# VectorE exp as a sum of four shifted bit patterns, two-tile ScalarE steps, and three shared PSUM banks, in a fused attention and feed-forward kernel

## The chip, the cores and the metric

One core of a Trainium2 chip runs the whole program. The metric is the device time of one execution in microseconds (us); several executions are taken and their median is given. The kernel before takes 830.55 us (three runs, 829.79 to 830.59). Each execution also has the mean clock that was granted to TensorE, as a share of full speed, and a state: fast, or slow when it is over 1.5% above the fastest run of the same kernel. Comparisons below are of fast runs, unless a line says otherwise.

## The reference, cut to what matters

```python
xn = _layernorm(x)                                  # x: 1 x 2048 x 640
q = (xn @ wq) -> 32 heads of 20; k = xn @ wk; v = xn @ wv     # one k and v for all heads
p = softmax(einsum("bhqd,bkd->bhqk", q, k) * 20 ** -0.5)
attention = (p @ v) @ wo
h = relu(xn @ w1 + b1); ffn = (h * h) @ w2 + b2               # 640 -> 1536 -> 640
return x + attention + ffn
```

The dominant work is exp of 32 x 2048 x 2048 scores. The kernel cuts it into 2,048 tiles of 128 x 512 (keys x queries of one head).

## The kernel before

ScalarE computes exp with its own function for most tiles. VectorE takes the rest and approximates exp through the bits of a bf16 number: a scaled score plus an offset, written as uint16 and read as bf16, is a piecewise linear 2^x. The kernel before corrects that line with a quadratic in the mantissa, in passes over four tiles (128 x 2048) at a time, called a set:

```python
# before, one set (L: bits of four tiles; n: number of the set)
d1   = DVE: lbuf[u16] = score * XA + XB                 # 4 times, from PSUM, 128x512
wop  = DVE: wbuf[u16] = (L & 0xFF80) | 124              # 128x2048
uop  = DVE: ubuf[u16] = (L & 0x7F) | 0x3F80
t1   = DVE: T = L * ubuf
t2   = DVE or (every other set) POOL in two halves: T = T * ubuf
# value products: 3 matmul groups a set: (lbuf, v), (wbuf, 0.5 v), (T, 0.164 v)

ACT_BANKS = ((0, 1, 2), (3, 4))   # ScalarE steps: 3 tiles, 2 tiles, 3 tiles, ...
DBANKS = (5,)                     # scores for VectorE
PVB = 6                           # value products
MB = 7                            # everything else ("misc": projections, feed-forward, output)
SQ (square of the feed-forward): POOL
```

The order of instructions on every engine is not written by hand. At build time a planner in the kernel simulates the engines with a duration for every operation, and emits what it would start first; on the chip each engine is given its list in that order, with semaphores. When the plan has nothing for TensorE it puts in fillers (matmuls with a zero weight, which add nothing), to keep TensorE's clock up:

```python
# for each engine: the ready operations; the earliest start wins, then priority
if pick[2].eng == "PE":
    while pick[0] > free["PE"] + 0.1 + ... and pe_credit(free["PE"]) < 0.0:
        commit(Op("fill", "PE", 0.215, [... zeros32 ...]))     # pe_credit falls with FILL * time
```

In row tiling (scores: contraction over 20 rows, four heads in four row tiles) and in column tiling (all else: 32 output columns, four column tiles) TensorE does up to four small matmuls at a time, a column group (in the timeline of the kernel before, at 401.57 us, four that start together are done in 0.39 us; one alone, at 407.72 us, takes 0.38). Matmuls write to PSUM, which the kernel uses as eight banks of 128 x 512. (`...` marks cuts.)

The softmax here doesn't subtract the row's maximum and nothing guards it: scores larger than these inputs give would overflow.

Of the kernel before, what the change touches and what calls it, by code (L numbers as in the profile page):

```python
# [13 lines left out]
HPG = 4  # L14
G = H // HPG
NBLK = QC * G
NQS = 4
# [8 lines left out]
CC = 0.1640625  # L26
LOG2K = -1.1033179
XA = SCALE * 1.4426950408889634 * 128.0
XB = (127.0 - EXP_SHIFT * 1.4426950408889634 + LOG2K) * 128.0

PTR = 20
ACT_BANKS = ((0, 1, 2), (3, 4))
DBANKS = (5,)
# [3 lines left out]
T2POOL = (0, 1)  # L37
DLEAD = 14.0
DGAP = 0.5
SWITCH = 0.1  # L40
FILL = 0.7

# [48 lines left out]

class Op:
# [3 lines left out]
    def __init__(self, name, eng, dur, parts, deps=(), toks=(), lat=0.06, lock=False, mode="C"):  # L96
        self.name, self.eng, self.dur, self.parts = name, eng, dur, parts
        self.deps = [d for d in deps if d is not None]
        self.toks = list(toks)
        self.lat, self.lock, self.mode = lat, lock, mode  # L100
        self.start = self.fin = None
        self.consumed = False
        self.tgt = None
        self.clock = None

    def ready(self):
        t = 0.0
        for d in self.deps:
            if d.fin is None:
                return None  # L110
            t = max(t, d.fin + d.lat)
        return t


def bass_parallel_sum__grouped_kv_mqa__dense_activation_squared_relu__prompt_kernel(nc, A_x, A_wq, A_wk, A_wv, A_wo, B_x, B_w1, B_b1, B_w2, B_b2, out):
    es = ExitStack()
    with es:
# [11 lines left out]
        stats6 = sb("stats6", [128, ST, 2, 6], F32)  # L129
# [11 lines left out]
        vxh = sb("vxh", [128, KT, 32], BF16)  # L141
        vxc = sb("vxc", [128, KT, 32], BF16)
# [3 lines left out]
        T2 = sb("T2", [128, 2, 512], BF16)  # L146
        OTn = sb("OTn", [128, 2, G, 512], BF16)
# [6 lines left out]
        ones0 = sb("ones0", [128, 128], BF16)  # L154
# [3 lines left out]
        part = sb("part", [128, 4, D], F32)  # L158
# [3 lines left out]
        tbuf = sb("tbuf", [128, 2, SETW], BF16)  # L162

        xfree = x_sb[:, :, :].rearrange("p st d -> p (st d)")
        lbuf = xfree[:, 0:2 * SETW].rearrange("p (a n) -> p a n", a=2)
        wbuf = xfree[:, 2 * SETW:4 * SETW].rearrange("p (a n) -> p a n", a=2)
        ubuf = sb("ubuf", [128, 2, SETW], BF16)
# [220 lines left out]
        def em_pool_consts():  # L388
            add(P.pool, lambda e: e.memset(ones0[:], 0.0), inc=c_pool)
            add(P.pool, lambda e: e.memset(ones0[0:1, :], 1.0), waits=[(c_pool, c_pool.n)], inc=c_pool)  # L390
# [182 lines left out]
        def add_scaled_v(c):  # L573
            cs = slice(4 * c, 4 * c + 4)
            d_, t_ = need_chunk(4 * c, v_op)
            o1 = Op(f"VH{c}", "POOL", 0.25, [lambda e: e.tensor_scalar(out=vxh[:, cs, :], in0=vx[:, cs, :], scalar1=0.5, scalar2=None, op0=ALU.mult)], d_, t_, lock=True)
            o2 = Op(f"VC{c}", "POOL", 0.25, [lambda e: e.tensor_scalar(out=vxc[:, cs, :], in0=vx[:, cs, :], scalar1=CC, scalar2=None, op0=ALU.mult)], d_, t_, lock=True)
            pool_q.extend([o1, o2])
            vs_op[c] = (o1, o2)
# [10 lines left out]
        mb_last = [None]  # L590

        def col4(lhs, rhs, n, k, last, m=32, bank=MB):
            return [mm(ps[32 * j:32 * j + m, bank, 0:n], lhs(j), rhs, k == 0, last, (0, 32 * j)) for j in range(4)]

        def unit_T(st):
            def chunk():
                return [(lambda e, dt=dt: e.transpose(out=psbf(MB)[:, dt * 128:(dt + 1) * 128], in_=xn_sb[:, st, dt * 128:(dt + 1) * 128], identity=ident[:])) for dt in range(DT)]  # L597

            def evac(p):
                o = Op(f"TE{st}", "DVE", 0.49, [lambda e: e.tensor_copy(out=xnT[:, :, st * 128:(st + 1) * 128],  # L600
                                                                        in_=psbf(MB)[:, 0:DT * 128].rearrange("p (dt n) -> p dt n", dt=DT))], [p])
# [4 lines left out]
        def unit_KT(c):  # L606
# [3 lines left out]
            def evac(p):  # L610
                o = Op(f"KTe{c}", "DVE", 0.75, [lambda e: e.tensor_scalar(out=kT[:, 512 * c:512 * (c + 1)], in0=ps[:, MB, :], scalar1=nk0[:, 1:2], scalar2=None, op0=ALU.add)],  # L611
# [5 lines left out]
        def unit_V(c):  # L617
            sts = range(4 * c, 4 * c + 4)

            def chunk():  # L620
                r = []
                for st in sts:
                    for dt in range(DT):
                        r.append(lambda e, st=st, dt=dt: e.matmul(ps[:, MB, DH * (st % 4):DH * (st % 4) + DH], xnT[:, dt, st * 128:(st + 1) * 128], wv_c[:, dt, :],  # L624
# [3 lines left out]
            def evac(p):  # L628
                o = Op(f"Ve{c}", "DVE", 0.24, [lambda e: e.tensor_copy(out=vx[:, 4 * c:4 * c + 4, 0:DH], in_=ps[:, MB, 0:4 * DH].rearrange("p (t d) -> p t d", t=4))],
# [7 lines left out]
        def unit_B1():  # L637
            def evac(p):
                b1_ev[0] = Op("B1e", "DVE", 0.17, [lambda e: e.tensor_copy(out=b1col[:], in_=psbf(MB)[:, 0:FT])], [p])
                return b1_ev[0]  # L640
            return Unit("B1", [(0.2, lambda: [lambda e: e.transpose(out=psbf(MB)[:, 0:FT], in_=b1row[:, :], identity=ident[0:FT, 0:FT])])],
                        lambda: True, evac, lambda: [], [(b1_sem, 16), (c_pool, v_ident)])

        def unit_QT(b):
# [5 lines left out]
            def evac(p):  # L650
                o = Op(f"QTe{b}", "DVE", 0.66, [lambda e: e.tensor_copy(out=qT[:, b % NQS, :], in_=ps[:, MB, :])], [p] + list(q_users.get(b - NQS, [])))  # L651
# [8 lines left out]
        def unit_FFN1(qc, f):  # L660
# [4 lines left out]
            def evac(p):  # L665
                k = nffn[0]
                nffn[0] += 1
                o = Op(f"RL{qc}_{f}", "DVE", 0.75, [lambda e: e.tensor_scalar(out=hT_tmp[:, k % 2, :], in0=ps[:, MB, :], scalar1=b1col[:, f:f + 1], scalar2=0.0,  # L668
# [8 lines left out]
                q = Op(f"SQ{qc}_{f}", "POOL", 1.15, [lambda e: e.tensor_tensor(out=h2T[:, qc % 2, f, :], in0=hT_tmp[:, k % 2, :], in1=hT_tmp[:, k % 2, :], op=ALU.mult)], dp, tk, lock=True)  # L677
                ffn_sq.append(q)
                sq_op[(qc, f)] = q
                pool_q.append(q)  # L680
# [5 lines left out]
        def out_mats(qc, st, half, gs, with_ffn):  # L686
# [3 lines left out]
            if with_ffn:  # L690
                for f in range(FT):
                    mats.append((h2T[:, qc % 2, f, stl * 128:(stl + 1) * 128], w2_sb[:, f, cs]))
                mats.append((ones0[:, :], b2pad[:, cs]))
# [4 lines left out]
        def out_chunks(mats, bank=MB, first=True, last=True):  # L698
            n = len(mats)
            ch = []  # L700
            for k, (l, r) in enumerate(mats):
                kk = k if first else k + 1
                ch.append((0.14, (lambda kk=kk, k=k, l=l, r=r: col4(lambda j: l[:, 32 * j:32 * j + 32], r, 320, kk, last and k == n - 1, 32, bank))))
# [22 lines left out]
        def unit_OUT(qc, st, half):  # L726
# [3 lines left out]
            def evac(p):  # L730
                o = Op(f"OE{st}_{half}", "DVE", 0.49, [lambda e: e.tensor_tensor(out=out_sb[:, slot, cs], in0=ps[:, MB, 0:320], in1=xr[:, slot, cs], op=ALU.add)],  # L731
# [13 lines left out]
        def unit_OUTP(st, half):  # L745
# [3 lines left out]
            def evac(p):  # L749
                o = Op(f"OP{st}_{half}", "DVE", 0.49, [lambda e: e.tensor_tensor(out=part[:, st % 4, cs], in0=ps[:, MB, 0:320], in1=xr[:, st % 4, cs], op=ALU.add)],  # L750
# [46 lines left out]
        act_tiles = []  # L797
# [6 lines left out]
        sets, steps = [], []  # L804

# [19 lines left out]
        def blk_qk_done(b):  # L825
            return cur["b"] > b and all(not (s["b"] == b and s["left"]) for s in sets) and all(st_["qk"].fin is not None for st_ in steps if any(t[0] == b for t in st_["tiles"]))

        def make_step():
            j = len(steps)
            banks = ACT_BANKS[j % 2]  # L830
            tl, (b1_, kt1, h1), rest = peek_tiles(len(banks))
            if not tl or not all(kt_ok(kt) and (b == 0 or b in qt_op) for b, kt, h in tl):
                return None
            cur["b"], cur["kt"], cur["h"] = b1_, kt1, h1
            for b, r in rest.items():
                unclaimed[b] = r
            i0 = len(act_tiles)
            st_ = dict(j=j, tiles=tl, banks=banks, i0=i0, act=None)
            steps.append(st_)
            act_tiles.extend(tl)  # L840
            parts, deps, toks = [], [], []
            for k, (b, kt, h) in enumerate(tl):
                for d_, t_ in (need_chunk(kt, kt_op), need_q(b)):
                    deps += d_
                    toks += t_
                parts.append(mm(ps[:, banks[k], :], kT[32 * h:32 * h + DH, kt * 128:(kt + 1) * 128], qT[32 * h:32 * h + DH, b % NQS, :], True, True, (32 * h, 0)))
            if j < 2:
                toks += all_pro
            st_["qk"] = Op(f"QK{j}", "PE", 0.215, parts, deps, toks, lat=0.2, mode="R")
            for (b, kt, h) in tl:  # L850
                q_users.setdefault(b, []).append(st_["qk"])
            return st_

        def act_can(st_):
            return all(i < PTR or act_tiles[i - PTR][:2] in pv_of for i in range(st_["i0"], st_["i0"] + len(st_["tiles"])))

        def make_act(st_):
            i0, n = st_["i0"], len(st_["tiles"])
            s0 = i0 % PTR
            deps = [st_["qk"]] + [pv_of[act_tiles[i - PTR][:2]] for i in range(i0, i0 + n) if i >= PTR]  # L860
            b0 = st_["banks"][0]
            return Op(f"ACT{st_['j']}", "ACT", 0.064 + 0.4267 * n, [lambda e: e.activation(out=PT[:, s0:s0 + n, :], in_=ps[:, b0:b0 + n, :], func=AF.Exp, bias=-EXP_SHIFT, scale=SCALE)], deps)  # L862

        def after_act(st_):
            for k, t in enumerate(st_["tiles"]):
                tile_act[t] = (st_["act"], (st_["i0"] + k) % PTR)
# [5 lines left out]
        def make_pv(b, kt):  # L872
# [11 lines left out]
            return Op(f"PV{b}_{kt}", "PE", 0.215, parts, deps, toks, lat=0.2)  # L884

        def make_dpv(s):
            b, kt, term, n = s["b"], s["kt"], s["term"], s["n"]
            first, last = b not in pv_begun, pv_count[b] == KT - 1 and term == 2
# [407 lines left out]
```

## Time and profile before

| | before |
|---|---|
| median | 830.55 us |
| span of the profiled run | 840.8 us |
| score tiles on ScalarE / VectorE | 1,696 / 352 |
| ScalarE exp steps | 339 of three tiles, 339 of two, 1 of one |
| filler matmuls | 1,088 |

In the views PE is TensorE, PEld its weight loads, DVE is VectorE, ACT ScalarE and POOL GpSimd; L12 is line 12 of the kernel. The profiled run of the kernel before is one of its longer ones (clock 0.962), so its span is above the median. From the page of the kernel before: busy time of each engine with its share of the span; TensorE's granted clock in 40 slices, in tenths; the chain that ended last.

```profile
PE 775.6 (92%) x10439; PEld 254.9 (30%) x10439; DVE 678.5 (81%) x973; ACT 794.5 (94%) x724; POOL 268.4 (32%) x168
...
PEclk8689999987989999999999999999999999999999
...
ACT 61%; PE 28%; DVE 6%; issue 1%; DVEq 0%
```

ScalarE is the bound, with TensorE next. Groups of the same page follow: line, engine, operation, what it writes and reads, count | busy us, mean ns of one | idle us of the engine just before it, and what ended that.

```profile
L862 ACT ACTIVATE PT<-ps 128x1536 bf16<-128x1536 f32 (+1 forms) x679 | 775.0, 1294 | 29.3 <-PE ps L549 27.5
...
L978 DVE TENSOR_SCALAR x_sb<-ps 128x512 uint16<-128x512 f32 x352 | 241.3, 685 | 113.2 <-PE ps L549 110.7
...
L549 PE MATMUL ps<-kT,zeros 128*32 128x512 bf16 x1088 | 87.9, 401 | 0.0
...
L985 DVE TENSOR_SCALAR x_sb<-x_sb 128x2048 uint16<-128x2048 uint16 x88 | 68.6, 780 | 0.5
```

The exp group is 775 us busy with 29 us of idle time before it. Mean durations overlap (the next step starts before the last one has ended), so I used start-to-start times: 1.330 us for three tiles, 0.903 us for two.

Two more lines are from the views of two lines of the source: GpSimd's own work with one input. Columns: engine, operation, tiles, count, duration in ns least/median/longest, first and last start, form.

```profile
L307 POOL TENSOR_SCALAR big<-x_sb,rstd,nmr x9: 868/874/1034, 10.4 to 23.5; 128x640 bf16<-128x640 bf16 x9
```

```profile
L576 POOL TENSOR_SCALAR vxh<-vx x4: 527/528/612, 28.8 to 58.7; 128x128 bf16<-128x128 bf16 x4
```

The first is the normalisation, the second one multiplication by a constant, at widths of 640 and 128.

### The profile page before, as it was taken

How to read it: one execution, taken by the hardware profiler on the slowest of the kernel's cores; microseconds unless marked ns; L12 is line 12 of the kernel's file. 1: busy time of each engine (PE TensorE's matmuls, PEld its weight loads, DVE VectorE, ACT ScalarE, POOL GpSimd, SP SyncE). 2: the span in 40 equal slices, each digit the busy share in tenths (PEclk: the TensorE clock that was granted, in tenths of full speed). 3: DMA queues.
4: the chain of work that ended last, by engine and by line, in shares of the span. 5: the costliest groups of instructions: out<-in, count | busy, mean ns of one | idle time of the engine just before them, and what ended most of it. 6: DMA issues, size and time to landing. Idle time of an engine off the chain costs nothing.

```text
span 840.8 us, 22953 instructions
## 1 busy us (share of the span) xinstructions
PE 775.6 (92%) x10439; PEld 254.9 (30%) x10439; DVE 678.5 (81%) x973; ACT 794.5 (94%) x724; POOL 268.4 (32%) x168
## 2 busy tenths in 40 slices
PE   7799999999999999899999999999899999999996
PEld 3232222222223333222223333322222333323332
DVE  5768888776878888889887877889888888888874
ACT  7589999997989999999999999999899999999995
POOL 4424344531222321254432223135343232223221
PEclk8689999987989999999999999999999999999999
DMA  9500000000000000000000000000000000000000
GB/s 306 120 2 2 1 2 2 2 2 1 2 2 17 3 17 18 17 2 2 2 2 2 17 18 17 3 16 2 2 2 2 18 17 18 17 2 2 3 2 33
DMA packets 11714, 14.94 MB, mean 18 GB/s; under 512 B 2017, under 2 KB 10978, under 8 KB 11618
## 3 DMA queue, kind: packets, MB, share of 16 engines
q1 hardware_dynamic: 10306, 13.44, 5.2%
q8 instruction: 81, 1.33, 0.7%
q10 hardware_dynamic: 1312, 0.05, 0.1%
q14 instruction: 15, 0.12, 0.0%
HBM read 10.87 MB, written 2.62 MB: 16 GB/s over the span
## 4 chain that ended last, share of the span: by engine, by line
ACT 61%; PE 28%; DVE 6%; issue 1%; DVEq 0%
ACT PT L862 61%; PE ps L549 28%; DVE x_sb L978 2%; DVE tbuf L989 1%; DVE T L914 1%; DVE ubuf L987 1%; DVE x_sb L985 0%; DVE hT_tmp L668 0%; PE ps L597 0%; DVE out_sb L1171 0%; DVE Tn L912 0%; DVE qT L651 0%; DVE kT L611 0%; DVE OTn L918 0%; PE ps L624 0%
## 5 line engine op out<-in xcount | busy, mean ns | idle before, releaser
L862 ACT ACTIVATE PT<-ps 128x1536 bf16<-128x1536 f32 (+1 forms) x679 | 775.0, 1294 | 29.3 <-PE ps L549 27.5
L549 PE MATMUL ps<-qT,kT 20*128 20x512 bf16 x2048 | 309.7, 393 | 46.3 <-ACT PT L862 33.1
L994 POOL TENSOR_TENSOR tbuf<-tbuf,ubuf 128x1024 bf16<-128x1024 bf16 x88 | 191.6, 2197 | 448.5 <-DVE tbuf L989 448.5
L978 DVE TENSOR_SCALAR x_sb<-ps 128x512 uint16<-128x512 f32 x352 | 241.3, 685 | 113.2 <-PE ps L549 110.7
L549 PE MATMUL ps<-PT,vx 128*32 128x512 bf16 x1696 | 171.1, 397 | 3.3 <-DVE Tn L912 3.1
L549 PEld LDWEIGHTS ps<-qT,kT 20*128 20x128 bf16 x2048 | 75.2, 91 | 313.6 <-ACT PT L862 234.3
L989 DVE TENSOR_TENSOR tbuf<-x_sb,ubuf 128x2048 bf16<-128x2048 bf16 x88 | 113.4, 1289 | 0.6
L549 PE MATMUL ps<-kT,zeros 128*32 128x512 bf16 x1088 | 87.9, 401 | 0.0
L677 POOL TENSOR_TENSOR big<-hT_tmp 128x512 bf16<-128x512 bf16 x48 | 58.1, 1216 | 90.2 <-DVE hT_tmp L668 90.1
L549 PEld LDWEIGHTS ps<-PT,vx 128*32 128x32 bf16 x1696 | 43.3, 93 | 108.4 <-issue 99.1
L549 PE MATMUL ps<-xnT,w_sb 128*32 128x512 bf16 x960 | 72.1, 381 | 1.6 <-DVE hT_tmp L668 1.0
L549 PE MATMUL ps<-w_sb,big 128*32 128x320 bf16 x1536 | 72.8, 301 | 0.8 <-DVE qT L651 0.4
L985 DVE TENSOR_SCALAR x_sb<-x_sb 128x2048 uint16<-128x2048 uint16 x88 | 68.6, 780 | 0.5
L987 DVE TENSOR_SCALAR ubuf<-x_sb 128x2048 uint16<-128x2048 uint16 x88 | 66.4, 755 | 0.0
L996 DVE TENSOR_TENSOR tbuf<-tbuf,ubuf 128x2048 bf16<-128x2048 bf16 x44 | 55.5, 1261 | 0.0
L549 PE MATMUL ps<-wo_pad,OTn 128*32 128x320 bf16 x1024 | 51.2, 300 | 0.7 <-DVE OTn L918 0.7
L549 PE MATMUL ps<-xnT,wq_sb 128*20 128x512 bf16 x620 | 47.4, 388 | 0.2 <-DVE out_sb L731 0.2
L549 PEld LDWEIGHTS ps<-w_sb,big 128*32 128x32 bf16 x1536 | 36.8, 96 | 26.4 <-issue 11.6
L668 DVE TENSOR_SCALAR hT_tmp<-ps,b1col 128x512 bf16<-128x512 f32 x48 | 35.7, 743 | 7.5 <-PE ps L549 7.2
L549 PE MATMUL ps<-x_sb,vx 128*32 128x512 bf16 x352 | 35.8, 397 | 0.8 <-DVE Tn L912 0.8
L549 PE MATMUL ps<-x_sb,vxh 128*32 128x512 bf16 x352 | 35.4, 393 | 0.0
L549 PE MATMUL ps<-tbuf,vxc 128*32 128x512 bf16 x352 | 35.2, 390 | 0.1
(84 smaller groups left out, 363.5 us busy)
## 6 DMA issues: line engine op xcount, KB each, us to landing
w_sb<-in_B_w_dram SPq DMA_DIRECT2D x2, 1920.0 KB, 10.7
xr<-in_A_x_dram SPq DMA_DIRECT2D x16, 160.0 KB, 2.4
out_dram<-out_sb SPq DMA_DIRECT2D x16, 160.0 KB, 1.8
x_sb<-in_A_x_dram SPq DMA_DIRECT2D x3, 640.0 KB, 7.6
wq_sb<-in_A_wq_dram SPq DMA_DIRECT2D x1, 800.0 KB, 10.5
wo_pad<-in_A_wo_dram SPq DMA_DIRECT2D x4, 200.0 KB
x_sb<-in_A_x_dram SPq DMA_DIRECT2D x2, 320.0 KB, 3.7
wk_c<-in_A_wk_dram ACTq DMA_DIRECT2D x1, 25.0 KB, 3.4
```

The source lines that it names most:

```text
L549: return lambda e: e.matmul(out_, l, r, start=start, stop=stop, tile_position=tp)
L668: o = Op(f"RL{qc}_{f}", "DVE", 0.75, [lambda e: e.tensor_scalar(out=hT_tmp[:, k % 2, :], in0=ps[:, MB, :], scalar1=b1col[:, f:f + 1], scal ...
L677: q = Op(f"SQ{qc}_{f}", "POOL", 1.15, [lambda e: e.tensor_tensor(out=h2T[:, qc % 2, f, :], in0=hT_tmp[:, k % 2, :], in1=hT_tmp[:, k % 2, : ...
L862: return Op(f"ACT{st_['j']}", "ACT", 0.064 + 0.4267 * n, [lambda e: e.activation(out=PT[:, s0:s0 + n, :], in_=ps[:, b0:b0 + n, :], func=AF ...
L914: tm = Op(f"TM{b}", "DVE", 0.69, [lambda e: e.tensor_tensor(out=T2[:, a, :].rearrange("p (c d) -> p c d", d=32), in0=Tn[:, a, :].rearrange ...
L978: d1 = dv(f"D1_{n}_{i}", 0.686, lambda e: e.tensor_scalar(out=lbuf[:, a, cs].bitcast(U16), in0=ps[:, bank, :], scalar1=XA, scalar2=XB, op0 ...
L985: s["wop"] = [dv(f"W{n}", 0.74, lambda e: e.tensor_scalar(out=W.bitcast(U16), in0=L.bitcast(U16), scalar1=0xFF80, scalar2=124, op0=ALU.bit ...
L987: s["uop"] = dv(f"U{n}", 0.74, lambda e: e.tensor_scalar(out=ubuf[:, a, :].bitcast(U16), in0=L.bitcast(U16), scalar1=0x7F, scalar2=0x3F80, ...
L989: s["t1"] = [dv(f"T1_{n}", 1.235, lambda e: e.tensor_tensor(out=T, in0=L, in1=ubuf[:, a, :], op=ALU.mult), [s["uop"]] + ([("pv", old, 2)] ...
L994: s["t2"].append(dv(f"T2_{n}", 2.15, lambda e, ks=ks: e.tensor_tensor(out=T[:, ks], in0=T[:, ks], in1=ubuf[:, a, ks], op=ALU.mult), s["t1" ...
L996: s["t2"].append(dv(f"T2_{n}", 1.235, lambda e: e.tensor_tensor(out=T, in0=T, in1=ubuf[:, a, :], op=ALU.mult), s["t1"], 4))
```

## The change

The intent: make a VectorE tile cheaper, so that VectorE can take more tiles from ScalarE. Four copies of the piecewise linear exp, their bit patterns shifted by 0, 32, 64 and 96, added with the weights 1, 0.84, 0.71 and 0.59, are meant to follow exp far more closely than one copy. The weights go into the values (the matmul does the sum), and each copy costs one addition to a uint16. Half of these passes are given to GpSimd. The core of the diff:

```diff
-ACT_BANKS = ((0, 1, 2), (3, 4))
-DBANKS = (5,)
+ACT_SIDES = ((0, 1), (2, 3))          # ScalarE steps of two tiles
+SHARED = (4, 5, 7)                    # VectorE scores and misc
+NSET = 3                              # sets in flight (2 before)
+PASS = (("DVE", "POOL", "POOL"), ("DVE", "POOL", "DVE"))
+LATS = {("PE", "ACT"): 0.215, ("PE", "DVE"): 0.215, ("ACT", "PE"): 0.21, ...}   # order model
 ...
-            s["wop"] = [dv(f"W{n}", 0.74, ... bitwise_and, bitwise_or ...)]
-            s["uop"] = dv(f"U{n}", 0.74, ... bitwise_and, bitwise_or ...)
-            s["t1"] = [dv(f"T1_{n}", 1.235, ... tensor_tensor mult ...)]
-            pool = T2POOL[n % len(T2POOL)]
-            ... s["t2"] ...
+            for j in range(1, NTERM):
+                T = tb(n, j)
+                eng = PASS[n % len(PASS)][j - 1]
+                p = dv(f"P{j}_{n}", 0.60 if eng == "DVE" else 1.9, lambda e, T=T, j=j: e.tensor_scalar(out=T.bitcast(U16), in0=L.bitcast(U16), scalar1=TSTEP * j, scalar2=None, op0=ALU.add), ...)
 ...
-                q = Op(f"SQ{qc}_{f}", "POOL", 1.15, ...)
+                q = Op(f"SQ{qc}_{f}", "DVE", 0.34, ...)
 ...
+            if o.eng == "POOL" and o.lock and last_lock[0] is not None and last_lock[0] not in o.deps:
+                o.deps.append(last_lock[0])
```

The number 1.9 in the last but two hunk is the planner's duration of a GpSimd pass. By the instruction order the changed kernel has 784 two-tile exp steps (1,568 tiles), 120 sets (480 tiles), 180 passes on VectorE, 180 on GpSimd, and 76 filler matmuls. The first 30 us come from a randomised search whose order can differ from build to build; the loop after it has the same order in every build.

## The prediction

> **What bounds the kernel now.** ScalarE does the exp of 1,696 of the 2,048 score tiles (128x512); VectorE does 352. The page gives ScalarE 94% busy, TensorE 92%, VectorE 81%, GpSimd 32%; the chain that ended last is 61% ScalarE exp and 28% TensorE. In back-to-back stretches of the timeline a three-tile exp starts its successor 1.330 us later and a two-tile exp 0.903 us later: 339 of each are 757 us. The loop runs from 31.8 to 831.7 us of the 840.8 us span, so ScalarE waits only about 42 us in it, nearly all of it after two-tile steps (the other bank pair has just 0.90 us for: release, scores, release). TensorE is less full than it looks: 1,088 of its matmuls (272 column groups of 0.215 us, 58 us) are zero fillers.
>
> **What the change does.** By the instruction order: ScalarE gets 784 two-tile steps (1,568 tiles), VectorE 480 tiles in 120 sets.
> - ScalarE: 784 x 0.903 = 708 us, 49 us less.
> - VectorE, by start-to-start times: the four passes per set (88 x 0.60, 88 x 0.60, 88 x 1.13, 44 x 1.13, about 255 us) become 180 one-op passes, which I cost like the present 128x2048 uint16 pass (0.60): 108 us. PSUM reads rise from 352 to 480 x 0.60 (+77 us), 48 squares come over from GpSimd (about +16 us). Net about 55 us less. It was not the bound.
> - GpSimd: 180 passes over 128x2048. My estimate from its tensor_scalar (128x128 0.53 us, 128x640 0.87 us) is 1.8 us each, about 330 us in all, against 250 us of products and squares now. The Trainium skill, "SBUF — State Buffer", section "Who interferes with whom", says that a VectorE op in a two-port mode and a GpSimd op block each other fully; here the 0.68 us normalise op has a mean of 880 ns and a longest of 2.5 us, which agrees. So VectorE will show some 2 us passes.
> - TensorE: fillers 1,088 to 76 matmuls (-54 us); value products of VectorE sets 264 to 480 column groups (+46 us), of ScalarE tiles 424 to 392 (-7 us); visits to row tiling 677 to 776. A visit costs 0.42 us where 0.215 us is the matmul: the Trainium skill, "TensorEngine Tiling (Array Packing)", section "Key Properties", says a mode change drains the array, and the trace agrees. Summed by these durations the loop needs about 698 us of TensorE, of which 694 real, against 690 now, of which 632 real.
>
> **Consequence.** The floor of ScalarE (708) falls, but TensorE's real work (694) rises to meet it: per ScalarE step of 0.903 us TensorE has 0.89 us of work, and every step now has the short window. I expect ScalarE to wait about 55 us in the loop (70 ns a step; the two-tile steps of now wait about 90 on average, 45 in the quiet stretches), so a loop near 763 us. With 32 us ahead, 9 after, and about 8 us that the timed runs are shorter than the profiled one: **797 us**, 4% faster; eight times in ten between 779 and 818. Chances: faster by over 2% 0.80, within 2% 0.17, slower 0.03.
>
> **What would show it.** Two-tile exps at 0.90 us start to start; ScalarE busy 710 to 730 us (the union of its spans); TensorE over 90% busy nearly without fillers; VectorE 550 to 610 us busy; GpSimd passes near 1.9 us; the chain of waits with more TensorE than 28%. Wrong if: GpSimd's uint16 pass takes 2.5 us or more, so that the sets lag and VectorE is locked out; TensorE cannot be packed over 90% and ScalarE waits 100 us (then within 2%); or the three shared banks hide so much that ScalarE waits under 35 us (then near 775).

(The normalise operation that it names reads two inputs. The operations of one input and 2,048 columns, which the change multiplies, show the same in that trace: L985's take 0.685 us in the median and 2.41 us at the longest, and the seven of 88 that were clearly held up all ended about 0.55 us after a GpSimd operation did.)

## The result, and the profile after

The changed kernel is right, and takes 1,311.26 us (median of four runs, 1,306.47 to 1,316.07, all fast), against 830.57 us of the kernel before beside it. The ratio is 1.574, with a 95% interval of 1.562 to 1.586: 57% slower where I had forecast 4% faster. A ratio here is the mean time of one kernel's fast runs over that of the other's in the same rounds, so it is not quite the ratio of the medians quoted.

The busy line and the chain of the page of the changed kernel:

```profile
PE 1140.5 (87%) x10168; PEld 259.6 (20%) x10168; DVE 890.1 (68%) x1020; ACT 803.6 (62%) x831; POOL 990.1 (76%) x213
...
PE 51%; POOL 25%; DVE 19%; issue 3%; POOLq 0%; ACT 0%; DVEq 0%
```

And in place of its row of the clock, two stretches (us, then busy us and count of PE, PEld, DVE, ACT and POOL; the next column is TensorE's mean granted clock):

```profile
300.00:500.00 200.00, 180.82 (x1607) 40.47 (x1607) 151.83 (x152) 127.04 (x127) 171.29 (x32) 0.60 0.02 6
...
700.00:900.00 200.00, 175.33 (x1603) 40.78 (x1603) 133.06 (x140) 122.20 (x122) 156.57 (x30) 0.61 0.03 8
```

ScalarE, the bound before, is idle for 38% of the span. GpSimd is 990 us busy, three times what I had costed, and TensorE's clock lies near 0.6. The groups say what GpSimd does:

```profile
L908 ACT ACTIVATE PT<-ps 128x1024 bf16<-128x1024 f32 x784 | 783.4, 1028 | 481.3 <-PE ps L564 480.5
...
L1044 POOL TENSOR_SCALAR tmore<-x_sb 128x2048 uint16<-128x2048 uint16 x60 | 323.1, 5395 | 95.8 <-DVE tmore L1044 62.4
L1044 POOL TENSOR_SCALAR tmore<-tmore 128x2048 uint16<-128x2048 uint16 x60 | 324.4, 5417 | 84.1 <-DVE tmore L1035 42.2
L1044 POOL TENSOR_SCALAR x_sb<-x_sb 128x2048 uint16<-128x2048 uint16 x60 | 323.1, 5396 | 83.3 <-DVE x_sb L1035 31.0
...
L564 PE MATMUL ps<-tmore,vxs 128*32 128x512 bf16 x960 | 124.6, 556 | 68.4 <-POOL tmore L1044 64.9
...
L1044 DVE TENSOR_SCALAR x_sb<-x_sb 128x2048 uint16<-128x2048 uint16 x60 | 116.5, 1948 | 0.4
L1044 DVE TENSOR_SCALAR tmore<-x_sb 128x2048 uint16<-128x2048 uint16 x60 | 114.0, 1911 | 0.5
L1044 DVE TENSOR_SCALAR tmore<-tmore 128x2048 uint16<-128x2048 uint16 x60 | 107.6, 1805 | 0.3
```

A GpSimd pass lasts 5.37 us (median), not 1.8 or 1.9: 180 of them are 966 us, more than the whole kernel before. VectorE's pass of the same shape has a median of 0.69 us, but a mean of 1.8 to 1.9: it is being held up. The timeline shows one such place (start, us, engine, line, operation; x2 is two instructions merged; between the rows lie those of other engines):

```profile
703.91 10.70 POOL L1044 TENSOR_SCALAR x_sb<-x_sb 128x2048 uint16<-128x2048 uint16 x2 [2.33 <-DVE x_sb L1035]
...
711.59 4.15 DVE L1044 TENSOR_SCALAR tmore<-tmore 128x2048 uint16<-128x2048 uint16 x2
...
717.03 5.37 POOL L1044 TENSOR_SCALAR tmore<-x_sb 128x2048 uint16<-128x2048 uint16 x1 [2.43 <-DVE tmore L1044]
...
718.72 4.23 DVE L1044 TENSOR_SCALAR tmore<-x_sb 128x2048 uint16<-128x2048 uint16 x1
```

VectorE's pass of 718.72 ends at 722.95, about 0.55 us after GpSimd's of 717.03 (which ended at 722.40): as if it did its work only when the other was done. The Trainium skill, "SBUF — State Buffer", section "Who interferes with whom", says that a VectorE operation in a two-port mode and a GpSimd operation exclude each other for the whole instruction; the trace agrees: 85 of VectorE's 180 passes began during a GpSimd pass, and all 85 ended 0.54 to 0.66 us after that pass did, while none of the other 95 took over 0.70 us. Summed, VectorE's 180 passes are 338 us busy where 180 x 0.69 would be 125.

So there is a first reading: the passes are late, everything that stands behind them in a fixed order waits (ScalarE 480 us for TensorE), and TensorE's clock falls besides. How much of this is the late result of a pass and how much the hold on VectorE was not separated. The page cannot say why a pass takes 5.37 us, whether the new order would have worked otherwise, or how much the clock does by itself.

### The profile page after: what moved, and what is told of

Its sections match the earlier page's. It is cut to its first block, busy times and chain, and to the rows that moved or that the text cites. A ratio compares the mean times of both kernels' runs of the same rounds, so it can differ in the third digit from the quotient of the medians.

```text
span 1304.7 us, 22593 instructions
## 1 busy us (share of the span) xinstructions
PE 1140.5 (87%) x10168; PEld 259.6 (20%) x10168; DVE 890.1 (68%) x1020; ACT 803.6 (62%) x831; POOL 990.1 (76%) x213
## 4 chain that ended last, share of the span: by engine, by line
PE 51%; POOL 25%; DVE 19%; issue 3%; POOLq 0%; ACT 0%; DVEq 0%
PE ps L564 51%; POOL tmore L1044 16%; POOL x_sb L1044 8%; DVE tmore L1044 7%; DVE x_sb L1044 4%; DVE x_sb L1035 4%; DVE tmore L1035 2%; DVE T L963 1%; DVE big L705 1%; DVE Tn L961 0%; POOLq L135 0%; DVE OTn L967 0%; DVE hT_tmp L696 0%; DVE qT L679 0%; DVE out_sb L1243 0%
## 5 line engine op out<-in xcount | busy, mean ns | idle before, releaser
L908 ACT ACTIVATE PT<-ps 128x1024 bf16<-128x1024 f32 x784 | 783.4, 1028 | 481.3 <-PE ps L564 480.5
L564 PE MATMUL ps<-qT,kT 20*128 20x512 bf16 x2048 | 437.1, 543 | 25.1 <-DVE x_sb L1035 15.1
L1044 POOL TENSOR_SCALAR tmore<-x_sb 128x2048 uint16<-128x2048 uint16 x60 | 323.1, 5395 | 95.8 <-DVE tmore L1044 62.4
L1044 POOL TENSOR_SCALAR tmore<-tmore 128x2048 uint16<-128x2048 uint16 x60 | 324.4, 5417 | 84.1 <-DVE tmore L1035 42.2
L1044 POOL TENSOR_SCALAR x_sb<-x_sb 128x2048 uint16<-128x2048 uint16 x60 | 323.1, 5396 | 83.3 <-DVE x_sb L1035 31.0
L564 PE MATMUL ps<-tmore,vxs 128*32 128x512 bf16 x960 | 124.6, 556 | 68.4 <-POOL tmore L1044 64.9
L1035 DVE TENSOR_SCALAR tmore<-ps 128x512 uint16<-128x512 f32 x160 | 106.4, 683 | 72.8 <-PE ps L564 72.3
L1044 DVE TENSOR_SCALAR tmore<-x_sb 128x2048 uint16<-128x2048 uint16 x60 | 114.0, 1911 | 0.5
L1044 DVE TENSOR_SCALAR tmore<-tmore 128x2048 uint16<-128x2048 uint16 x60 | 107.6, 1805 | 0.3
L564 PE MATMUL ps<-x_sb,vxs 128*32 128x512 bf16 x480 | 64.2, 561 | 33.0 <-POOL x_sb L1044 32.1
```

Source lines behind the costliest of these rows:

```text
L564: return lambda e: e.matmul(out_, l, r, start=start, stop=stop, tile_position=tp)
L908: return Op(f"ACT{st_['j']}", "ACT", 0.05 + 0.4267 * n, [lambda e: e.activation(out=PT[:, s0:s0 + n, :], in_=ps[:, b0:b0 + n, :], func=AF. ...
L1035: d1 = dv(f"D1_{n}_{i}", 0.60, lambda e: e.tensor_scalar(out=L[:, cs].bitcast(U16), in0=ps[:, bank, :], scalar1=XA, scalar2=XB, op0=ALU.mu ...
L1044: p = dv(f"P{j}_{n}", 0.60 if eng == "DVE" else 1.9, lambda e, T=T, j=j: e.tensor_scalar(out=T.bitcast(U16), in0=L.bitcast(U16), scalar1=T ...
```

## The experiments

Fourteen kernels were run. Theory A: the length of GpSimd's pass is the whole cause, and the rest of my sum holds. Rival B: the order itself cannot run (TensorE has 0.89 us of work per 0.90 us exp step; two banks a side), and the pass only adds to it. Rival C: blocking on the port is what hurts, whatever the length.

### e_alone: the pass by itself

A small kernel that only runs GpSimd operations, six of each form, on buffers that nothing else uses.

> No attention at all: the output is a copy of x, wrong on purpose. GpSimd runs eleven forms of pass by themselves, six times each, nothing else touching its memory but one copy of x in and out. Theory 'the pass itself is slow': the uint16 add over 128x2048 takes 5.3 to 5.4 us here too, and half and a quarter of the width about 2.7 and 1.4 us. Rival 'it is slow only because VectorE keeps it off the shared port': about 1.9 us alone. If the type is at fault, the bf16 forms of the same width take 1.8 to 2.8 us; if every one-input form of that width takes over 5 us, it is not the type. A 1024-element int32 tensor_tensor add, which does two uint16 adds in each element, should take 2.1 to 2.4 us, like the bf16 product of that width (2.12 us in the kernel before).

Groups of its trace (the first is the pass in question):

```profile
L57 POOL TENSOR_SCALAR dst<-src 128x2048 uint16<-128x2048 uint16 x6 | 32.2, 5369 | 0.5
L69 POOL TENSOR_SCALAR dst<-src 128x2048 bf16<-128x2048 bf16 x6 | 32.2, 5366 | 0.5
...
L61 POOL TENSOR_SCALAR dst<-src 128x1024 uint16<-128x1024 uint16 x6 | 16.6, 2769 | 0.5
...
L77 POOL TENSOR_SCALAR dst<-src,sc 128x2048 bf16<-128x2048 bf16 x6 | 12.3, 2052 | 0.6
L97 POOL COPY dst<-src 128x2048 uint16<-128x2048 uint16 x6 | 11.4, 1894 | 0.4
L85 POOL TENSOR_TENSOR dst<-src,ci 128x1024 int32<-128x1024 int32 x6 | 11.4, 1892 | 0.5
L65 POOL TENSOR_SCALAR dst<-src 128x512 uint16<-128x512 uint16 x6 | 8.9, 1489 | 0.5
L105 DVE TENSOR_SCALAR dst<-src 128x2048 uint16<-128x2048 uint16 x6 | 4.2, 694 | 222.5 <-POOL dst L97 222.3
```

The pass takes 5.37 us with nothing beside it, so VectorE's hold on the port does not explain its length. The type is not at fault either: a bf16 product by a constant (L69) takes the same. But L77, bf16 times one column plus another column, does the same width in 2.05 us, and a plain copy (L97) in 1.89. L69 and L77 are the two forms that I had mixed: the uint16 points of 512, 1024 and 2048 columns lie on a line of about 0.2 us plus 2.5 ns a column, which gives 0.52 us at 128 columns, close to the 0.53 of L576 in the kernel before; the 0.87 us at 640 columns of L307 belongs to the other form.

### e_short and e_i32: the same order with a short pass

e_short lets GpSimd touch only 704 columns (wrong); e_i32 computes the right result in another form, two uint16 at a time. The loop's order is that of the changed kernel in both: in the traces of after, e_short, e_i32, e_col and e_ma (the last two come below) every engine starts the same sequence of instructions from 32 us on.

```diff
 e_short
-  out=T.bitcast(U16), in0=L.bitcast(U16), scalar1=TSTEP * j, op0=add
+  out=T[:, 0:704].bitcast(U16), in0=L[:, 0:704].bitcast(U16), scalar1=TSTEP * j, op0=add      # GpSimd alone
 e_i32
+  cadd = sb("cadd", [128, NTERM], I32)          # both halves hold 32 j
+  e.tensor_tensor(out=T.bitcast(I32), in0=L.bitcast(I32), in1=cadd[:, j:j + 1].to_broadcast([128, SETW // 2]), op=ALU.add)
```

> The changed kernel in its very order, but GpSimd's passes touch only 704 of 2048 columns, about 1.85 us each, near the 1.9 us that the order was planned for (plus one memset of the buffers at the start, so that nothing unwritten is read). Wrong result on purpose. Theory A (the length of GpSimd's pass is the whole cause): about 800 us, 785 to 820, clock back above 0.9. Rival B (the order itself cannot run: TensorE has 0.89 us of work per 0.90 us exp step, only two banks a side, shared banks): above 870 us even so.

> The changed kernel in its very order, right result: GpSimd adds the shift to two uint16 at a time, as an int32 tensor_tensor add of 128x1024 with a broadcast column of constants (no carry crosses, since no sum reaches 65536). Expected pass 2.1 to 2.4 us. Theory A: 795 to 825 us. Rival B: above 870 us.

The views of the line of the passes, e_short and then e_i32:

```profile
L1045 POOL TENSOR_SCALAR x_sb<-x_sb x60: 1969/1970/1975, 38.3 to 723.9; 128x704 uint16<-128x704 uint16 x60
```

```profile
L1048 POOL TENSOR_TENSOR x_sb<-x_sb,cadd x60: 1892/1892/1895, 39.1 to 796.6; 128x1024 int32<-128x1024 int32 x60
```

The passes took 1.97 and 1.89 us (I had expected 1.85, and 2.1 to 2.4). e_short: one fast run of 765.85 us, three slow ones of 796.61 to 804.19. e_i32: two fast ones of 775.64 and 782.83, two slow ones of 838.67 and 854.95; ratio of the fast runs 0.934 (0.925 to 0.944). So the very order that took 1,311 us takes under 785 when the pass is short. B falls; its 870 us is not reached even by a slow run. The fast runs lie below A's ranges too (785 to 820, and 795 to 825): my sum had too much waiting in it, see below. Of e_short's page (its fast run):

```profile
PE 743.2 (97%) x10164; PEld 227.4 (30%) x10164; DVE 613.6 (80%) x1022; ACT 738.8 (97%) x830; POOL 374.1 (49%) x213
```

TensorE and ScalarE are both 97% busy: the two can be packed far tighter than I had believed.

### e_dve: all passes on VectorE

```diff
-PASS = (("DVE", "POOL", "POOL"), ("DVE", "POOL", "DVE"))
+PASS = (("DVE", "DVE", "DVE"),)
```

> The change with all three passes of each set on VectorE, GpSimd idle in the loop; order planned anew by the kernel's own planner (still 784 exp steps and 120 sets). VectorE gains 180 passes of 0.6 us, so about 660 us busy, and no port conflict remains. Theory A: 790 to 820 us. Rival B: above 870 us. A third theory, that blocking on the shared port and not the length of GpSimd's pass is what hurts, also gives 790 to 820 us here but would leave e_i32 well slower than this run.

One fast run of 768.59 us, three slow ones of 792.69 to 804.28; VectorE 696 us busy in the profiled (slow) run, where I had expected 660. It is on A's side, though below its 790 to 820. As e_i32 is near it, blocking on the port matters little once the passes are short, and C falls as the main cause.

### e_form, e_col, e_warm: which form is slow

My second theory was that a constant in the instruction is what makes it slow, and a column of constants fast.

```diff
 e_col (e_warm: the same, and 24 useless full matmuls before the loop)
+  ccol = sb("ccol", [128, NTERM], F32)
   # and the first 30 us pinned: the search goes through its tasks in sorted order
-  scalar1=TSTEP * j
+  scalar1=(ccol[:, j:j + 1] if eng == "POOL" else TSTEP * j)
```

> No attention: output is a copy of x, wrong on purpose. Seven more forms of GpSimd's tensor_scalar by themselves, six times each. The first such run gave 5.37 us for one constant in the instruction, of uint16, bf16 and f32 alike at 2.5 ns an element, but 2.05 us for bf16 with two columns of scalars. Theory 'a constant in the instruction is what is slow': uint16 with one column scalar takes 2.0 to 2.1 us (1024 wide about 1.1), and two constants stay at 5.3 us or more. Rival 'one operation is slow, two are fast': one column scalar 5.4 us, two constants 2.05 us.

> The changed kernel with one thing different in the loop: GpSimd's pass takes its shift from a column of f32 constants in memory instead of from the instruction (three memsets at the start; the order of the first 30 us, which otherwise differs from build to build, pinned). Right result. If constants in the instruction are the slow form, passes of about 2.05 us and 765 to 785 us in fast runs, with some runs 20 to 80 us longer where TensorE's clock is granted half speed at the loop's start. If not, 1,250 us or more.

> e_col with 24 matmuls of the whole array, of no use and without a wait, put just before the loop. The slow runs of the repaired kernels began the loop at half clock and stayed there for 75 to 109 us. If it is the state at the loop's start that decides this, all runs here lie within 760 to 785 us. If the loop itself lets the clock fall, runs stay spread up to 800 us and more as in e_col.

The theory fell: e_col took 1,324.47 us (ratio 1.592), e_warm 1,318.46 (ratio 1.582), with passes of 5.44 us in both; e_warm's question about the clock could not be answered in a kernel still held up by its passes. Groups of e_form, in the order of their lines in the program: one column scalar (L57); 1,024 wide (L61); two constants, add and add (L65); two constants, multiply and add, bf16 (L69); one column, multiply, bf16 (L73); two columns, add and add (L77).

```profile
L77 POOL TENSOR_SCALAR dst<-src,sc 128x2048 uint16<-128x2048 uint16 x6 | 43.4, 7234 | 0.6
L65 POOL TENSOR_SCALAR dst<-src 128x2048 uint16<-128x2048 uint16 x6 | 42.5, 7085 | 0.5
L73 POOL TENSOR_SCALAR dst<-src,sc 128x2048 bf16<-128x2048 bf16 x6 | 32.6, 5439 | 0.6
L57 POOL TENSOR_SCALAR dst<-src,sc 128x2048 uint16<-128x2048 uint16 x6 | 32.6, 5436 | 0.6
...
L69 POOL TENSOR_SCALAR dst<-src 128x2048 bf16<-128x2048 bf16 x6 | 11.4, 1898 | 0.5
```

Of the arithmetic forms tried, what is fast is one pair of operations, multiply then add, about as fast as the copy; a single operation takes 2.8 times as long, and add-then-add is slower still. Why was not found.

### e_ma: the pass as multiply-then-add

```diff
-  e.tensor_scalar(out=T.bitcast(U16), in0=L.bitcast(U16), scalar1=TSTEP * j, scalar2=None, op0=ALU.add)
+  e.tensor_scalar(out=T.bitcast(U16), in0=L.bitcast(U16), scalar1=1.0, scalar2=float(TSTEP * j), op0=ALU.mult, op1=ALU.add)   # GpSimd alone
   # and the first 30 us pinned, as in e_col
```

> My theory that a constant in the instruction is the slow form fell: a column scalar took 5.44 us too. What was fast among the forms run alone is the pair multiply-then-add (1.90 us with two constants, 2.05 us with two columns, bf16); single operations and add-then-add took 5.4 to 7.2 us. So here GpSimd's pass is written as times 1.0, plus the shift; the sums stay whole numbers under 65536. Right result. If the pair of operations decides, the uint16 pass takes about 1.9 us and fast runs 765 to 785 us. Rival: the fast form is one for bf16 alone; then the pass takes over 5 us and the time is 1,300 us or more. Prologue pinned, no warm-up.

From the view of that line in e_ma:

```profile
L1044 POOL TENSOR_SCALAR x_sb<-x_sb x60: 1899/1901/1904, 39.9 to 781.3; 128x2048 uint16<-128x2048 uint16 x60
```

The pass takes 1.90 us, for uint16 too: multiplying by one makes it 2.8 times as fast. Three fast runs of 774.97 to 775.18 us, three slow ones of 796.59 to 823.42; ratio of the fast runs 0.926 (0.914 to 0.938). The result is right. e_col is the control: with the same pinned start, the same order of the loop and a slow form of the pass (5.44 us) it took 1,324 us. This settles the cause: with one operation added to one instruction, 57% slower becomes 7% faster.

### e_told: the slow pass, planned for

```diff
-  p = dv(f"P{j}_{n}", 0.60 if eng == "DVE" else 1.9, ...)
+  p = dv(f"P{j}_{n}", 0.60 if eng == "DVE" else 5.37, ...)
```

> The changed kernel with its slow pass as it is, but the planner told that it lasts 5.37 us: it then takes 88 sets rather than 120, 848 exp steps, and 334 column groups of fillers. Exp floor 848 x 0.903 = 766 us, GpSimd 132 x 5.37 = 709 us. If the harm came from an order planned for passes that were in truth 2.8 times as long (waits in order on every engine), the time falls to 815 to 870 us, not far from the kernel before, with the very same slow instruction. If such a pass harms whatever the plan (through the port it holds), above 950 us.

One fast run of 918.75 us, three slow ones of 937.80 to 952.62, which lies between my two expectations. Planning with the true duration wins back about 390 of the 480 us, with the same slow instruction in it 132 times. But the new plan is another one in more than its order: it takes 88 sets, not 120, and so gives GpSimd 48 passes less (258 us at 5.37 us each), and it puts in 1,336 fillers. How much is the order alone was not separated. And it does not win back all: this kernel is still 80 us slower than the one before beside it (838.76 us). The page of its profiled run (a slow one) has ScalarE waiting 124 us for TensorE. What those 80 us are, I have not separated.

### e_fill and e_fill2: how much is the clock

```diff
+  # before a value product that waits for a GpSimd pass
+  for _ in range(8):        # e_fill2: 2
+      commit(Op("fill", "PE", 0.0, [... zeros32 ...]))
```

> The changed kernel, its slow passes left as they are, with eight column groups of zero fillers (1.7 us at full clock) before each value product that waits for a GpSimd pass, so that TensorE works where it waited; about 310 us of extra work. If half of the loss is the half-speed clock that the waits bring, the clock rises above 0.85 and the time falls to 1,020 to 1,150 us, near GpSimd's own 966 us of passes plus its waits. If the passes' length alone makes the time, 1,290 us or more.

> The changed kernel, slow passes as they are, with two column groups of fillers (0.43 us at full clock, 77 us in all) before each value product that waits for a GpSimd pass, where eight gave 1,351 us at a mean clock of 0.855. If the half-speed clock is a large part of the loss in its own right, a cheaper dose brings the time below 1,250 us. If the waits for late passes set the time and the clock only follows, 1,290 to 1,350 us again.

e_fill: 1,350.78 us at a mean clock of 0.855. e_fill2: 1,262.77 us at 0.758. (One run each, of unknown state; the changed kernel has 1,311.26 at 0.60 to 0.62.) e_fill came out on the side of the passes' length (1,290 or more), e_fill2 between its two expectations. With the large dose the clock rose by more than a third and the time did not fall, but some 310 us of useless work (my estimate before the run) had gone in with it; with the small one some 49 us were won. So the low clock costs time of its own, at least these 49 us; how much, the two runs do not measure. It need not be little: TensorE is busy for 1,140.5 us with 10,168 matmuls in the changed kernel, and for 753.0 us with 10,319 in e_mafill (below). That the clock is low at all follows from the slow passes: e_short, in the same order, has 0.993 in its fast run. A part of the loss needs neither: 180 passes of 5.37 us hold GpSimd for 966 us in any order, 135 us more than the whole kernel before. How the rest divides between waits and clock stays open.

### e_i32w, e_mafill, e_dvefill: the slow runs of the repaired kernels, and a better version

The repaired kernels have slow runs which the kernel before hardly has. In all the traces the granted clock takes only two values, 0.5 and 1.0 (a window's mean can lie between); the Trainium skill, "TensorE: Matmul & The Clock Gate", section "What's actually happening", says so, and the trace agrees. The first trial was a warm-up before the loop:

```diff
 e_i32w (e_i32, first 30 us pinned)
         em_wo_late()
+        pe_dummies(24)
```

> e_i32 (passes of 1.89 us, so not hidden by slow passes) with the prologue pinned and 24 useless matmuls of the whole array just before the loop; the trial of this on e_col told nothing, since its passes were still slow. If the clock at the loop's start decides between fast and slow runs, all runs lie within 765 to 790 us; if not, they are spread up to 850 us as e_i32's were (775.6 to 855.0).

Two fast runs of 773.94 and 774.00 us, two slow ones of 790.79 and 815.18: still spread. Its fast run shows how the clock falls. Busy time in stretches, with columns as above:

```profile
190.00:200.00 10.00, 9.69 (x122) 2.45 (x114) 9.25 (x17) 10.00 (x12) 5.06 (x4) 1.00 0.01 2
200.00:207.00 7.00, 5.97 (x70) 1.50 (x67) 7.00 (x11) 7.00 (x9) 5.18 (x3) 0.99 0.00 0
207.00:212.00 5.00, 5.00 (x40) 1.01 (x36) 3.16 (x6) 4.02 (x5) 1.89 (x1) 0.50 0.00 0
...
230.00:240.00 10.00, 10.00 (x150) 3.11 (x146) 7.46 (x12) 9.64 (x11) 5.57 (x4) 0.96 0.02 3
```

After 7 us in which TensorE was 85% busy (5.97 of 7.00, no gap longer than 0.53 us; in the thinnest part, 203 to 206 us, 66%), the clock halves, and then stays so although TensorE is 100% busy. The same skill page, section "Why this matters for your kernels", asks for no gaps above about 3 us; here far less was enough. The profiled slow run of e_ma fell at the same place of the same order, with the same three short gaps (0.30, 0.20 and 0.53 us), and stayed low for 116 us. So I raised the planner's fill rate, which puts fillers into just such thin stretches:

```diff
 e_mafill (from e_ma), e_dvefill (from e_dve, pinned)
-FILL = 0.7
+FILL = 1.0
+        pe_dummies(24)
```

> e_ma (GpSimd pass as multiply-then-add, 1.90 us) with the warm-up of e_i32w and the planner's fill rate raised from 0.7 to 1.0, which sets 208 zero-filler matmuls where it set 76. In the fast run of e_i32w the clock fell at 207 us after 3 us in which TensorE waited for ScalarE. If thin stretches of the plan let the clock fall, fast runs come to 766 to 774 us and fewer than half of the runs are slow; if not, the spread stays 774 to 825 us.

> e_dve (all passes on VectorE) with the same warm-up and fill rate (216 filler matmuls where it had 88). Same question: 765 to 772 us in most runs if thin stretches let the clock fall; spread of 768 to 805 us if not. Against e_mafill it tells whether GpSimd at 1.90 us a pass is worth having at all: by the fast runs so far (768.6 against 775.0) VectorE alone is as good or better.

e_mafill: 766.18 us (766.07 to 766.63, five runs, all fast, clock 0.995); ratio 0.918 (0.913 to 0.923). e_dvefill: 768.18 us (767.82 to 768.59, six runs); ratio 0.920 (0.915 to 0.925). No slow run is left in either, for 132 and 128 filler matmuls more. Both are right, and both beat both kernels. Whether the fill rate alone does it was not tried; the warm-up alone did not, in e_i32w. Both ran on another chip than e_ma and e_dve, which were not run again beside them; the kernel before spread about as much there (830.62 to 842.99 us) as beside e_ma (830.71 to 844.78). From e_mafill's page:

```profile
PE 753.0 (98%) x10319; PEld 231.9 (30%) x10319; DVE 624.7 (82%) x1020; ACT 739.3 (97%) x831; POOL 359.8 (47%) x213
...
PEclk8999999999999999999999999999999999999999
...
L909 ACT ACTIVATE PT<-ps 128x1024 bf16<-128x1024 f32 x784 | 719.0, 1205 | 4.9 <-PE ps L565 4.8
```

ScalarE's idle time before its exp steps is 4.9 us where it was 481.3 in the changed kernel and 29.3 before. GpSimd at 1.90 us a pass gains 2 us over VectorE alone: it was hardly needed.

## Why the prediction was wrong, point by point

- **The step that failed** is the third of the list: "GpSimd: 180 passes over 128x2048. My estimate from its tensor_scalar (128x128 0.53 us, 128x640 0.87 us) is 1.8 us each, about 330 us in all". It measured 5.37 us each and 966 us in all, alone as in the kernel (e_alone). I drew a line through two points that belong to two forms of the instruction: the 0.53 us is one multiplication, the 0.87 us a multiply-and-add. The first point lies on the line of the one-operation form, which gives 5.3 us at 2,048 columns. That the planner holds 1.9 us for the pass made my number look confirmed; it was an assumption, not a measurement.
- I did name it as what would make me wrong ("GpSimd's uint16 pass takes 2.5 us or more, so that the sets lag and VectorE is locked out"), but left 0.03 for slower. The timeline shows that lockout; VectorE was 890 us busy where I had put 550 to 610 (624.7 in e_mafill).
- **ScalarE's floor** held: two-tile exps start 0.904 us apart at best in the changed kernel (0.903 in e_mafill), and 784 of them are 708 us.
- **TensorE's sum** (694 us of real work in the loop) was not contradicted. The loop of e_mafill lasts 719 us (31.9 to 751.0) and holds 208 fillers, 52 column groups or 11 us; so the real work in it is at most about 708 us.
- **ScalarE's waits** were sized too large. I put 55 us in the loop, its length less 784 x 0.903. By that measure e_mafill's loop has 11 us (the page's idle time, 4.9 us, is another measure: it counts only gaps between exps). So its loop is 44 us shorter than my 763; some 13 us come back after the loop and from the 8 us that I took off for the timed runs, since the profiled run of the kernel before was merely one of its longer ones. This is why the repaired kernel does not land at my 797 us but at 766 to 775. I had named the case: "the three shared banks hide so much that ScalarE waits under 35 us (then near 775)". I took the waits of the kernel before, whose order model has shorter latencies (0.06 us by default), for a property of the banks; the changed planner, with its new latencies and its shared banks, packs both engines to 97 or 98%. Which of these parts does it was not separated.
- **The mode change of TensorE** (0.42 us a visit) was needed for the sum; no later run disagrees with it.

## What to carry to other kernels

A duration belongs to the exact form of an instruction: engine, number and kind of operations, operand kinds, width; two points of different forms make no line, and a form that the trace does not hold deserves a run by itself before an order is planned on it. In a statically planned order one operation of wrong length is paid by every engine behind it (here ScalarE waited 480 us for TensorE), and by the clock; a planner's own table of durations is the first thing to check against a trace. When TensorE is nearly full, leave a few fillers in the thin stretches: here, with 132 more filler matmuls and a warm-up, none of five runs was slow, where three of six had taken 797 to 823 us.

## What the Trainium skill lacked or had wrong

- "GPSIMD Engine Reference", section "Engine selection", calls one-input work on GpSimd "roughly line-rate". Here a one-operation tensor_scalar over 128x2048 takes 5.37 us (uint16 or bf16, constant; 5.44 with a column), against 0.69 us on VectorE. The words fit only a copy (1.89 us) and multiply-then-add (1.90).
- No page that I looked up says that multiply-then-add is a fast form of it: 1.90 us with two constants, 2.05 with two columns, where one operation takes 5.37 and add-then-add 7.09 to 7.23.
- "GPSIMD Engine Reference", the same section: an exact int32 addition is named, but not its speed. Two uint16 additions at a time over 128x1024 int32 take 1.89 us, 2.8 times as fast as the uint16 form.
- "TensorE: Matmul & The Clock Gate", section "Why this matters for your kernels", warns of idle gaps above about 3 us. That is no safe limit here: in e_i32w the clock fell to 0.5 after 7 us at 85% busy with no gap over 0.53 us, and stayed there for 24 us although TensorE was busy all the time; in a slow run of e_ma it stayed for 116 us.
